# A fixed table for the issue order of all operations in an attention and FFN kernel on one core

## The chip, the cores and the metric

The kernel runs on one core of a Trainium2 chip. The metric is the device time in microseconds (us), median of three runs. A core has five engines with a queue each: TensorE (PE) for matrix products, VectorE (DVE), ScalarE (ACT), GpSimd (POOL), and SyncE (SP), which issues nearly all transfers here. An engine takes the instructions of its queue in order; between engines, semaphores hold an instruction back until what it reads is written and what it overwrites is read.

## What is computed

```python
def _attn_ref(q, k, v, tau):                      # 8 batches, 8 heads, 576 rows, head size 64
    scores = scale * np.matmul(q, k.transpose(0, 1, 3, 2))
    thresh = np.max(scores, axis=-1, keepdims=True) - tau
    scores = np.where(scores >= thresh, scores, -1000000000.0)
    scores = scores - np.max(scores, axis=-1, keepdims=True)
    attn = np.exp(scores)
    attn = attn / (np.sum(attn, axis=-1, keepdims=True) + 1e-09)
    return np.matmul(attn, v)
def _moe_ref(x, w_in, w_out, s, b):               # 4608 tokens, 512 -> 2048 -> 512
    r = np.maximum(x @ w_in, 0.0)
    return (s * (r * r) + b) @ w_out
```

The attention's output, heads side by side, is the x of the second part (the FFN).

## The kernel before

**Tiling.** A visit is one pair of heads of one batch and one part u of its query rows: 256 rows (u = 0) or 256 and the last 64 (u = 1). There are 64 visits, four (the four pairs) for each part. A visit has four score tiles of 128 rows by 576 keys, and a fifth for the last 64 rows. When the four pairs of a part are through, their values are 256 tokens of x and one FFN block runs: 16 steps f of 128 hidden units each. The last rows of four batches make a block of their own, so there are 18 blocks.

**A score tile** (`tile_of`): PE writes the products into a PSUM bank pair s0 or s1 (L427 for the first 12 visits, L438 from then on, L416 and L449 for the last rows); DVE scales them and takes the minimum (L472), DVE or ACT adds tau to it (L480, L477), ACT takes the exponential into em (L483), DVE masks and sums (L486) and takes the reciprocal of the sum (L491), POOL multiplies by it (L494; the first four visits do it behind the values, L573 and L596). The probabilities are transposed on PE in the first eight visits (L509, L512, then ACT copies them to er, L521 and L524), on DVE and by transfers later (L543, L545, L562). The values are 20 products of er with V (L582) into the bank pv, taken to x by ACT (L595, L599).

**An FFN block**: ACT and DVE split x into a high and a low part (L696, L698). Step f has 12 products h (L712, entries from L715 in two halves for f = 0 and 15), then on ACT a relu, a square and a rounding (L719, L720, L722), on POOL the low part (L723), and the second product in two halves, o0 and o1, of three matmuls each (L729). Both weight matrices are split into parts once, in the first 130 us (`weights`, L657 to L671), from loads L621 and L624. The column sums that carry b are one product (L676).

**The order.** Nothing is issued while these functions run: each call of `plan.add` makes an entry of what it emits, on which engine, with an assumed duration, and with the entries that it depends on. There are 6381 entries (PE 1314, DVE 1317, ACT 1891, POOL 791, SP 1067, one empty), numbered as they are added, and the numbers are the same before and after. `Plan.run` (L131 to L162) then makes the order in which they are issued, and so each engine's queue. It runs a list scheduler over the assumed durations forward, backward and forward again (`ordered`, L164 to L240), permutes the first 779 places by the table FIRST (L30), and moves 136 entries by the table MOVES (L65). Then the entries are emitted in that order (L899 to L902); waits follow from what each reads and writes.

Of the kernel before, what the change touches and what calls it, by code (L numbers as in the profile page):

```python
# [22 lines left out]
ROUNDS = 2  # L23
# [6 lines left out]
FIRST = (  # L30
# [33 lines left out]
)  # L64
# [21 lines left out]
class Plan:  # L86
# [44 lines left out]
    def run(self):  # L131
# [7 lines left out]
        for k in range(ROUNDS):  # L139
# [5 lines left out]
            if k == ROUNDS - 1:  # L145
                break
# [797 lines left out]
```

## Time and profile before

| | us |
|---|---|
| median of three runs | 1210.88 |
| lowest and highest | 1210.82, 1211.03 |
| span of the profiled execution, first to last instruction | 1208.6 |
| PE busy with matmuls | 1191.3 |
| DVE, ACT, POOL busy | 798.0, 763.4, 696.4 |

The profile is of one execution. The end of a matmul in it is modelled and consecutive matmuls overlap, so how fast PE moves is read from the starts of its instructions, and a shown idle time is the least that was lost. In a row of the timeline "x12" is a run of twelve like instructions; in brackets stands the idle time of the engine ahead of the row and what ended it.

### The profile page before, as it was taken

What the parts mean: (1) busy time and instruction counts of PE and PEld (TensorE: products, weight loads), DVE (VectorE), ACT (ScalarE), POOL (GpSimd) and SP (SyncE); (2) the same over time, 40 slices, a digit from 0 to 9 for tenths busy, and PEclk for the clock granted to TensorE, in tenths of its full rate; (3) what the DMA queues carried; (4) which work ended last, traced back from release to release, by engine and by line L of the source; (5) the groups of instructions that cost most, each with busy time, mean ns of one, the idle gap of its engine ahead of it and who ended that gap; (6) DMA issues with size and microseconds to landing.
All of it is one profiled execution on the core that took longest, in us unless ns stands there. A gap on an engine that the chain in (4) does not pass through costs nothing.

```text
span 1208.6 us, 24492 instructions
## 1 busy us (share of the span) xinstructions
PE 1191.3 (99%) x7956; PEld 985.4 (82%) x7956; DVE 798.0 (66%) x2149; ACT 763.4 (63%) x1890; POOL 696.4 (58%) x806
## 2 busy tenths in 40 slices
PE   7899999999999999999999999999999999999998
PEld 5577778788888888888887888788888888888997
DVE  7988876677786866766776667667766676672011
ACT  6888756666666766656666666566666566663443
POOL 2467636666666775566575666566657566562210
PEclk9999999999999999999999999999999999999999
DMA  8742465877867877666767776667767666762000
GB/s 298 260 136 80 97 157 133 182 181 170 186 150 179 187 159 171 150 159 151 171 142 163 177 160 143 155 146 162 163 159 164 156 154 152 169 148 57 17 18 18
DMA packets 259393, 180.68 MB, mean 149 GB/s; under 512 B 83394, under 2 KB 238018, under 8 KB 259266
## 3 DMA queue, kind: packets, MB, share of 16 engines
q1 hardware_dynamic: 259120, 178.98, 62.8%
q8 instruction: 64, 1.05, 0.3%
q14 instruction: 63, 0.52, 0.1%
q10 hardware_dynamic: 146, 0.13, 0.0%
HBM read 87.03 MB, written 9.44 MB: 80 GB/s over the span
## 4 chain that ended last, share of the span: by engine, by line
PE 96%; DVE 2%; DMA 1%; issue 0%; ACT 0%; POOL 0%; DVEq 0%; ACTq 0%; POOLq 0%
PE h L712 35%; PE o L729 34%; PE pv L582 13%; PE s L438 9%; PE s L427 2%; PE s L449 1%; PE pv L509 1%; DVE s L472 1%; DMA w<-in_moe_w_out_dram 1%; DMA vb<-in_v_dram 0%; PE s L416 0%; PE pv L512 0%; PE h L820 0%; DVE tr L486 0%; DVE k L662 0%
## 5 line engine op out<-in xcount | busy, mean ns | idle before, releaser
L712 PE MATMUL h<-xh,w 128*128 128x256 f32 x2304 | 465.5, 284 | 1.0 <-ACT g L719 0.9
L712 PEld LDWEIGHTS h<-xh,w 128*128 128x128 f32 x2304 | 377.4, 190 | 20.4 <-issue 2.6
L729 PE MATMUL o<-w,gh 128*128 128x512 f32 x1152 | 366.5, 399 | 0.0
L472 DVE TENSOR_SCALAR_CACHE_REDUCE s<-s,nsc 128x576 f32<-128x576 f32 x288 | 234.5, 821 | 144.4 <-PE s L438 115.4
L712 PE MATMUL h<-xl,w 128*128 128x256 f32 x1152 | 325.2, 282 | 0.6 <-DVE xl L698 0.6
L723 POOL TENSOR_TENSOR gl<-g,gh 128x256 fp32r<-128x256 f32 x272 | 204.0, 752 | 207.9 <-ACT gh L722 190.1
L494 POOL TENSOR_SCALAR em<-em,st,zero 128x576 f32<-128x576 f32 x262 | 219.2, 837 | 139.3 <-DVE st L491 89.9
L486 DVE SCALAR_TENSOR_TENSOR em<-s,st,em 128x577 f32<-128x577 f32 x270 | 218.4, 810 | 94.3 <-ACT st L477 59.5
L483 ACT ACTIVATE em<-s,st 128x576 f32<-128x576 f32 x270 | 199.0, 738 | 79.5 <-DVE s L472 50.1
L729 PEld LDWEIGHTS o<-w,gh 128*128 128x128 f32 x1152 | 194.9, 189 | 37.4 <-issue 15.9
L729 PE MATMUL o<-w,gl 128*128 128x512 f32 x576 | 224.8, 390 | 0.0
L712 PEld LDWEIGHTS h<-xl,w 128*128 128x128 f32 x1152 | 219.0, 190 | 6.6 <-DVE xl L698 0.8
L719 ACT ACTIVATE g<-h 128x256 f32<-128x256 f32 x288 | 110.4, 383 | 177.6 <-PE h L712 160.1
L543 DVE STREAM_TRANSPOSE tr<-em 128x512 f32<-128x512 f32 x252 | 178.2, 707 | 51.0 <-POOL em L494 43.9
L403 POOL TENSOR_TENSOR k<-kr,k 64x576 fp32r<-64x576 f32 x104 | 149.4, 1438 | 53.2 <-ACT k L402 40.0
L582 PE MATMUL pv<-er,vb 128*64 128x256 f32 (+1 forms) x1280 | 170.9, 412 | 0.4 <-ACT er L524 0.4
L438 PE MATMUL s<-k 128*128 128x288 f32 x832 | 144.1, 296 | 0.0
L438 PEld LDWEIGHTS s<-k 128*128 128x128 f32 x832 | 127.9, 188 | 17.6 <-issue 2.1
L582 PEld LDWEIGHTS pv<-er,vb 128*64 128x64 f32 x1280 | 86.5, 137 | 68.0 <-issue 14.2
L722 ACT CAST gh<-g 128x256 fp32r<-128x256 f32 x288 | 115.7, 404 | 34.1 <-PE o L729 30.3
L729 PEld LDWEIGHTS o<-w,gl 128*128 128x128 f32 x576 | 108.2, 188 | 25.0 <-POOL gl L723 0.3
L720 ACT ACTIVATE g<-g 128x256 f32<-128x256 f32 x288 | 119.7, 417 | 4.2
(104 smaller groups left out, 909.8 us busy)
## 6 DMA issues: line engine op xcount, KB each, us to landing
er<-tr SPq DMA_DIRECT2D x448, 160.0 KB, 3.5
kr<-in_k_dram SPq DMA_DIRECT2D x116, 288.0 KB, 4.3
vb<-in_v_dram SPq DMA_DIRECT2D x128, 128.0 KB, 3.3
qr<-in_q_dram SPq DMA_DIRECT2D x56, 160.0 KB, 4.5
er<-tr SPq DMA_DIRECT2D x112, 80.0 KB, 2.3
w<-in_moe_w_in_dram SPq DMA_DIRECT2D x16, 512.0 KB, 6.3
w<-in_moe_w_out_dram SPq DMA_DIRECT2D x16, 512.0 KB, 7.2
out_dram<-oo SPq DMA_DIRECT2D x30, 256.0 KB, 2.7
```

Source lines behind the costliest of these rows:

```text
L403: pool((1500, 1500), lambda: nc.gpsimd.tensor_tensor(out=z()[D:P], in0=kr[D:P, j], in1=z()[D:P].bitcast(F32), op=ALU.subtract), rk + [("z" ...
L438: nc.tensor.matmul(flat[sk][:, S0 + hf * HS:S0 + (hf + 1) * HS], lazy["q"][:, x, j, qc], lazy["k"][:, j, cs], start=(x == 0), stop=(x == 1))
L472: dve((740, 875), lambda: nc.vector.tensor_scalar(out=ps[:, S0:S0 + S], in0=ps[:, S0:S0 + S], scalar1=nsc, scalar2=None, op0=ALU.mult, op1 ...
L483: act((632, 740), lambda: nc.scalar.activation(out=ev, in_=ps[:, S0:S0 + S], func=AF.Exp, bias=low, scale=-1.0), [sk, (ks_, 0, k_)], [em_k ...
L486: dve((742, 830), lambda: nc.vector.scalar_tensor_tensor(out=eb, in0=ps[:, S0:S0 + S + 1], scalar=limit, in1=eb, op0=ALU.is_le, op1=ALU.mu ...
L494: pool((795, 825), lambda: nc.gpsimd.tensor_scalar(out=ev, in0=ev, scalar1=share, scalar2=zero, op0=ALU.mult, op1=ALU.add), [em_k, (ks_, 4 ...
L543: nc.vector.transpose(out=to[:, :, 0:NQ].rearrange("p m c q -> p m (c q)"), in_=ev[:, 0:M].rearrange("p (m r) -> p m r", m=4))
L582: nc.tensor.matmul(ps[j * D:(j + 1) * D, 0:32 * nb], vb[r, n, j, c], er[r, n, j, 0:nb, 32 * c:32 * c + 32], start=(c == 0), stop=(c == 4))
L712: nc.tensor.matmul(ps, w[:, c, :], x[:, c, :], start=(c == 0 and i == 0), stop=(c == NC - 1 and i == 2))
L720: act((322, 417), lambda: nc.scalar.activation(out=g, in_=g, func=AF.Square), [f"g{k}"], [f"g{k}"], at)
L723: do((712, 740), lambda: eng.tensor_tensor(out=lo, in0=g, in1=hi.bitcast(F32), op=ALU.subtract), [f"g{k}", f"gh{n}"], [f"gl{n}"], at)
L729: nc.tensor.matmul(bank[f"o{t}"], a[:, ts_], w, start=(f == 0 and i == 0), stop=(f == NF - 1 and i == 2))
```

## The change

The scheduler, both tables and the constants that it used go. A table ORDER names all 6381 entries in the order in which they are issued, and `run` returns them so. The entries, their engines, shapes and buffers are the same.

```diff
-import heapq
...
-ROUNDS = 2
...
-FIRST = (
-    1, 2, 3, 0, 7, 8, 9, 12, 13, 15, 16, 17, 18, 19, 20, 4, 22, 21, 25, 11, 6, 24, 26, 29, 31, 30, 33, 35, 36, 75, 14,
...
-MOVES = (
-    (780, 779), (1990, 2018), (2006, 2019), (2007, 2020), (2012, 2021), (2013, 2022), (4900, 4918), (4915, 4919),
...
+ORDER = (
+    1, 9, 2, 8, 7, 13, 14, 15, 16, 17, 18, 19, 20, 21, 22, 23, 24, 3, 10, 12, 40, 11, 41, 49, 42, 50, 0, 43, 44, 51, 52,
+    57, 190, 192, 193, 194, 27, 29, 30, 45, 58, 60, 66, 59, 67, 61, 139, 68, 69, 141, 142, 53, 54, 46, 47, 48, 78, 79,
...
     def run(self):
-        ops = self.ops
-        after = [[] for _ in ops]
...
-        return [ops[n][3] for n in order]
-
-    def ordered(self, before, after, rank, busy, done, back):
...
+        at = {n: k for k, n in enumerate(ORDER)}
+        assert len(at) == len(ORDER) == len(self.ops)
+        assert all(at[d] < at[n] for n in at for d in self.ops[n][4])
+        return [self.ops[n][3] for n in ORDER]
```

By engine, the entries that have another place in their queue than before, and the farthest move in places: PE 653 of 1314, 11; DVE 651 of 1317, 17; ACT 1015 of 1891, 32; POOL 400 of 791, 9; SP 641 of 1067, 43. On PE the changes between products on a part of the array (L427, L449, L582) and on the whole are 186 before and 182 after. The ends of the queues are the same, on PE the last 144 entries.

Some stretches of the queues, by entry number, before and after:

| queue, about when in the trace of before | before | after |
|---|---|---|
| POOL, start | 7, 8, 0 | 8, 7, 0 |
| SP, about 17 us | 280, 594, 204, 300, 136, ... (80 stood early, 138 later) | 280, 138, 80, 528, 299, ... |
| DVE, 48 to 59 us | 229, 237, 311, 322, 325, 323, 189, 544, 326, 238, 545, 534, 547, 535, 537, 538, 245, 555, 247, 548, 249 | 229, 237, 303, 322, 323, 189, 534, 238, 325, 544, 545, 535, 326, 547, 537, 538, 548, 245, 311, 247, 249, 555 |
| ACT, 56 to 60 us | 244, 246, 248, 541, 557, 344, 543, 252 | 244, 329, 246, 248, 541, 341, 543, 344, 557, 252 |
| PE, 56 to 61 us | 243, 554, 540, 250, 542, 251, 550, 258 | 243, 554, 540, 542, 250, 251, 550, 258 |
| PE, 133 to 148 us | 477, 497, 498, 780, 783, 512, 513, 961, 520, 518, 793, 519, 794, 801 | 498, 780, 477, 783, 512, 513, 961, 520, 497, 518, 793, 794, 519, 801 |
| PE, 213 to 217 us | 906, 1332, 1103, 1110, 1340 | 1103, 905, 898, 1110, 906, 1340 |

What they are: 7 the ones and zeros of PE's first products (L796, L797) and 8 the identity (L799); 80, 138 loads of V for visits 1 and 2 (L379, L382); 143, 196, 30, 303, 326 weight steps on DVE (L660, L662), 311 one of L671, 325 one of L660; 229 and 237 the masks L486 of the last tiles of visit 3 and 238 its reciprocal L491; 189 and 245 the values' scaling L596 of visits 2 and 3; 534, 544, 555 scale steps L472 of visit 4; 547, 537 its masks, 548 a reciprocal; 243 the values of visit 3, 244 its copy L595; 246, 248 the high parts L696 and 247, 249 the low parts L698 of the first block; 250, 251 the halves of its first product; 540, 542, 550 transposes L509 and L512 of visit 4, 541 and 543 their copies; 240 and 242 the last transpose of visit 3 and its copy L524; 780 a transpose L512 and 783 the values of visit 7; 477, 497, 498, 518, 519, 898, 905, 906 second-product halves L729; 520 the column sums L676; 793 and 794 the halves of the second block's first product and 801 its next product; 1103 and 1110 two products of the third block.

## Rows read from the trace of the kernel before

**Rows 1.** The page's first part: busy us of each engine, share, instructions.

```profile
PE 1191.3 (99%) x7956; PEld 985.4 (82%) x7956; DVE 798.0 (66%) x2149; ACT 763.4 (63%) x1890; POOL 696.4 (58%) x806
```

**Rows 2.** Busy time by stage: stretch, us, busy of PE, PEld, DVE, ACT, POOL, clock, DMA.

```profile
0.00:58.00 58.00, 46.48 (x291) 30.93 (x291) 49.56 (x141) 42.67 (x85) 20.18 (x29) 0.97 0.87 288
12.50:55.50 43.00, 35.59 (x245) 23.33 (x244) 42.90 (x118) 36.97 (x77) 16.27 (x13) 0.96 0.93 304
150.00:1150.00 1000.00, 999.53 (x6741) 837.23 (x6740) 659.46 (x1783) 625.07 (x1570) 612.36 (x706) 1.00 0.68 153
```

**Rows 3.** Timeline of PE in an undisturbed stretch: start, us, engine, line, operation, tiles, count.

```profile
605.80 0.63 PE L729 MATMUL o<-w,gh 128*128 128x512 f32 x2
...
606.49 0.28 PE L712 MATMUL h<-xh,w 128*128 128x256 f32 x1
...
607.93 0.63 PE L729 MATMUL o<-w,gh 128*128 128x512 f32 x2
```

**Rows 4.** Waits of PE's products from 58 us on: us in total, times, longest.

```profile
PE h L712 <- ACT g L719: 0.9, 2, 0.5
```

**Rows 5.** Timeline of PE, 134 to 149 us.

```profile
136.62 3.06 PE L582 MATMUL pv<-er,vb 128*64 128x320 f32 x20 [0.40 <-ACT er L524]
...
143.03 0.96 PE L729 MATMUL o<-w,gh 128*128 128x512 f32 x2
...
144.30 0.38 PE L712 MATMUL h<-xh,w 128*128 128x256 f32 x1
...
146.41 0.28 PE L712 MATMUL h<-xh,w 128*128 128x256 f32 x1
147.16 0.38 PE L712 MATMUL h<-xh,w 128*128 128x256 f32 x1 [0.47 <-ACT g L719]
```

**Rows 6.** Timeline of DVE, 49 to 53 us.

```profile
49.36 0.69 DVE L671 TENSOR_TENSOR bias_t<-bias_t,k 128x512 f32<-128x512 f32 x1
49.96 0.76 DVE L660 TENSOR_SCALAR k<-k 128x512 int32<-128x512 int32 x2
...
52.30 0.69 DVE L662 SCALAR_TENSOR_TENSOR k<-w,k 128x512 int32<-128x512 int32 x1
52.92 0.17 DVE L491 RECIPROCAL st<-st 128x4 f32<-128x4 f32 x1
```

**Rows 7.** Timeline of ACT, 52.8 us: the last copy of visit 3.

```profile
52.84 0.27 ACT L524 COPY er<-pv 64x128 f32<-64x128 f32 x1
```

**Rows 8.** Timeline of PE at the first FFN product.

```profile
57.89 0.36 PE L712 MATMUL h<-xh,w 128*128 128x256 f32 x1
58.88 0.39 PE L712 MATMUL h<-xl,w 128*128 128x256 f32 x1 [0.63 <-DVE xl L698]
```

**Rows 9.** Timeline of POOL at the start: the identity's first step, and what follows it.

```profile
1.13 0.21 POOL masks.py:197 MEMSET k<- 128x128 f32 x1
...
1.64 0.53 POOL L786 MEMSET bias_t<- 128x512 f32 x1
```

**Rows 10.** Timeline of PE, values of visits 0 and 1; the page's median landing of V loads.

```profile
22.70 2.48 PE L582 MATMUL pv<-er,vb 128*64 128x256 f32 x20
...
33.51 1.12 PE L573 MATMUL pv<-k,st 128*64 128x128 f32 x8
...
vb<-in_v_dram SPq DMA_DIRECT2D x128, 128.0 KB, 3.3
```

**Rows 11.** The page's costliest groups: count, busy us, mean ns, idle before.

```profile
L472 DVE TENSOR_SCALAR_CACHE_REDUCE s<-s,nsc 128x576 f32<-128x576 f32 x288 | 234.5, 821 | 144.4 <-PE s L438 115.4
L486 DVE SCALAR_TENSOR_TENSOR em<-s,st,em 128x577 f32<-128x577 f32 x270 | 218.4, 810 | 94.3 <-ACT st L477 59.5
L483 ACT ACTIVATE em<-s,st 128x576 f32<-128x576 f32 x270 | 199.0, 738 | 79.5 <-DVE s L472 50.1
```

**Rows 12.** Busy time in two stretches of the front, columns as in rows 2.

```profile
28.00:32.00 4.00, 2.09 (x17) 1.50 (x15) 4.00 (x13) 3.60 (x9) 2.87 (x3) 1.00 0.96 284
32.00:35.50 3.50, 3.50 (x22) 2.49 (x21) 3.50 (x7) 1.73 (x5) 0.00 (x0) 0.51 0.65 196
```

More of the change, by code (lines that the diff above doesn't have):

```diff
@@ L29 @@
 SCALED_LATE = 4
-FIRST = (
[33 rows of a table removed]
-)
-MOVES = (
[17 rows of a table removed]
+ORDER = (
[326 rows of a table added]
 )
 class Plan:
-    HANDOVER, TO_PE = 50, 150
-    PASS, OVER = 100, 400
-    TURN, NEAR = 95, 8000
-    SPARE = {"DVE": 100, "ACT": 100, "POOL": 100, "SP": 300}
-    SHARE, LATER, STRETCH, EARLY = 0.7, 1.0, 1.3, 75e3
     def __init__(self):
@@ L117, in banks @@
         return [k] if k in ("s0", "s1", "pv", "o0", "o1") else ["h"] if k in ("h0", "h1") else []
-    def free_at(self, n, t, last, tail, hand):
-        for b, writes in self.ops[n][8]:
-            for e, wrote, at, rest in last.get(b, ()):
-                if e != self.ops[n][0] and (writes or wrote):
-                    t = max(t, at + (rest if tail is None else tail) + hand)
-        return t
-    def used(self, n, at, rest, last):
-        for b, writes in self.ops[n][8]:
-            was = last.get(b, []) if not writes else []
-            last[b] = [u for u in was if u[1] or u[0] != self.ops[n][0]] + [(self.ops[n][0], writes, at, rest)]
@@ L131, in run @@
-    def run(self):
-        ops = self.ops
-        after = [[] for _ in ops]
-        for n, o in enumerate(ops):
-            for d in o[4]:
-                after[d].append(n)
-        before = [o[4] for o in ops]
-        rank, early = [o[5] for o in ops], set()
-        for k in range(ROUNDS):
-            more = [(self.SHARE if n in early else self.LATER) * self.SPARE.get(o[0], 0) +
-                    (self.STRETCH - 1) * o[1] * (o[0] == "PE" and n in early) for n, o in enumerate(ops)]
-            busy = [o[1] + s for o, s in zip(ops, more)]
-            done = [o[2] + s for o, s in zip(ops, more)]
-            order = self.ordered(before, after, rank, busy, done, False)
-            if k == ROUNDS - 1:
-                break
-            early = {n for t, n in order if t < self.EARLY}
-            end = {n: t + done[n] for t, n in order}
-            last = max(end.values())
-            back = self.ordered(after, before, [last - end[n] for n in range(len(ops))], busy, done, True)
-            start = {n: -t - done[n] for t, n in back}
-            rank = [start[n] for n in range(len(ops))]
-        order = [n for _, n in order]
-        order[:len(FIRST)] = [order[k] for k in FIRST]
-        moved = [(to, order[k]) for k, to in MOVES]
-        gone = {n for _, n in moved}
-        order = [n for n in order if n not in gone]
-        for to, n in moved:
-            order.insert(to, n)
-        at = {n: k for k, n in enumerate(order)}
-        assert len(at) == len(ops) and all(at[d] < at[n] for n in at for d in before[n])
-        return [ops[n][3] for n in order]
@@ L164, in ordered @@
-    def ordered(self, before, after, rank, busy, done, back):
-        ops = self.ops
-        left = [len(b) for b in before]
-        ready = [0.0] * len(ops)
-        free, coming, there = {}, {}, {}
-        for n, o in enumerate(ops):
-            free[o[0]] = 0.0
-            coming.setdefault(o[0], [])
-            there.setdefault(o[0], [])
-            if not left[n]:
-                heapq.heappush(coming[o[0]], (0.0, n))
-        order, port, mode, last = [], 0.0, False, {}
-        def delay(n, t):
-            at = max(t, port) if ops[n][6] else t
-            if not ops[n][8]:
-                return at - t
-            hand = self.TO_PE if ops[n][0] == "PE" else self.HANDOVER
-            return self.free_at(n, at, last, done[n] - busy[n] if back else None, hand) - t
-        for _ in ops:
-            best = None
-            for e in free:
-                t = free[e]
-                while coming[e] and coming[e][0][0] <= t:
-                    n = heapq.heappop(coming[e])[1]
-                    heapq.heappush(there[e], (rank[n], n))
-                if not there[e]:
-                    if not coming[e]:
-                        continue
-                    t = coming[e][0][0]
-                if best is None or t < best[0]:
-                    best = t, e
-            t, e = best
-            while coming[e] and coming[e][0][0] <= t:
-                n = heapq.heappop(coming[e])[1]
-                heapq.heappush(there[e], (rank[n], n))
-            n = heapq.heappop(there[e])[1]
-            if e == "PE" and mode and not ops[n][7]:
-                for at, m in sorted(there[e]):
-                    if ops[m][7] and at < rank[n] + self.NEAR:
-                        there[e].remove((at, m))
-                        heapq.heapify(there[e])
-                        heapq.heappush(there[e], (rank[n], n))
-                        n = m
-                        break
-            wait = delay(n, t)
-            if wait > self.PASS:
-                for at, m in sorted(there[e]):
-                    if delay(m, t) <= self.PASS and busy[m] < wait + self.OVER:
-                        there[e].remove((at, m))
-                        heapq.heapify(there[e])
-                        heapq.heappush(there[e], (rank[n], n))
-                        n, wait = m, delay(m, t)
-                        break
-            t += wait
-            if e == "PE":
-                t += self.TURN * (mode != ops[n][7])
-                mode = ops[n][7]
-            if ops[n][6]:
-                port = t + busy[n]
-            if ops[n][8]:
-                self.used(n, t + busy[n], done[n] - busy[n], last)
-            order.append((t, n))
-            free[e] = t + busy[n]
-            for u in after[n]:
-                if ops[u][0] == e == "PE":
-                    late = busy[n]
-                else:
-                    late = busy[n] + done[u] - busy[u] if back else done[n]
-                    p = n if back else u
-                    late += 0 if ops[u][0] == e else self.TO_PE if ops[p][0] == "PE" else self.HANDOVER
-                ready[u] = max(ready[u], t + late)
-                left[u] -= 1
-                if not left[u]:
-                    heapq.heappush(coming[ops[u][0]], (ready[u], u))
-        order.sort()
-        return order
```

372 rows, old and new, of tables (FIRST, MOVES, ORDER) are left out of this document.

## The prediction

> **What bounds the kernel now.** I read the page's busy line first: TensorE (PE) has matmuls running for 1191.3 of 1208.6 us, the other engines are at 66% and less [rows 1]. So only time in which PE does not run at its own pace can be won by an order, and the second view, busy time by stage, says where that is: up to 58 us PE is busy for 46.5 of 58.0 us, from 150 to 1150 us for 999.5 of 1000 [rows 2]. Third, the pace: in an undisturbed stretch the starts follow one another by 0.69 us for half of a second FFN product, 1.44 for a first product [rows 3]; no order changes these. Fourth, the list of waits behind 58 us: PE waits for ScalarE's L719 twice, 0.9 us together [rows 4]; beside it stand two waits of 0.6 and 0.4 us, which come below. The middle has therefore almost nothing to give, and the question is what the table does at a handful of places, and whether it opens new waits.
>
> Before 58 us the reader has to look at VectorE (DVE), not PE. From 12.5 to 55.5 us it is busy for 42.9 of 43.0 us [rows 2], and the FFN cannot start before the first four visits have passed through it; PE's stalls there are shadows of that chain. After 58 us everything to the end is PE work of fixed length. So the end moves by (1) how far the first FFN product moves, (2) the PE waits behind it that vanish, (3) those that appear. The median of the runs is 1210.88 us and the profiled execution's span 1208.6; I work on the span and keep the 2.3 us outside it.
>
> **Behind 58 us, what vanishes.** Four places, each read as start-to-start minus the pace.
> - 783, values of visit 7: PE is idle for 0.40 us because L582 waits for the last ScalarE copy (L524) of the transposes just ahead of it [rows 5]. In the new order 477, a second-product half of 0.69 us, stands between transpose 780 and 783. It covers the wait: 0.40.
> - 518 and 793 around the column sums (520, L676): 518 starts at 143.03 and 793 at 144.30, 1.27 us for a half worth 0.69, so 0.58 are lost [rows 5]. The new order puts 497 as well (0.69) between. Unknown is how much of the 0.58 is the full-precision sum itself still draining: bounds 0 and 0.58, I take 0.45, since the next consumer of the bank (793) is the one that stalls.
> - 801 behind 794: the last start of 794 at 146.41 and the first of 801 at 147.16, 0.75 where 0.12 is the spacing, so 0.63, released by L719 [rows 5]. In the new order 519 (0.69) stands between instead of ahead of 794: covered, 0.63.
> - 1110 directly behind 1103 at 216 us: the other of the two waits of [rows 4], also 0.63. The new order has 905 and 898 between, 1.38: covered.
> Sum 2.1 us, bounds 1.7 and 2.4. The work that moved there comes from places where it covered nothing I can find. PE changes between tiled and whole-array products 182 times instead of 186, worth under 0.1 us each by the same spacing; I count nothing.
>
> **The front.** The first FFN product needs the values of visit 3 (243, L573 and L582), whose last condition is the reciprocal 238 (L491 at 52.92 us); the last ScalarE copy 242 ends with it, at 53.10 [rows 6, 7]. On DVE the new table takes 311, 325, 326 and 544 from ahead of 238 and puts 534 there: by their spacing 0.60 + 0.38 + 0.62 = 1.60 us earlier, 544 and 534 being alike [rows 6]. But the copies hang on the mask 237, and only 303 (a step like 326, 0.62) leaves from ahead of it. So 243 moves by 0.6 to 1.5 us; I take 1.0, as two more DVE steps that release transposes (189, L596) also move. Then 247, the low part that 250 waits 0.99 us for (57.89 to 58.88 [rows 8]): 555 leaves from ahead of it (0.82, the L472 of [rows 11]), 311 enters (0.60) but starts at once, because 555 stood waiting for its scores; I take 0.5, bounds 0.2 and 1.0. Against this, transpose 542 now precedes 250, and needs a ScalarE copy that queues behind both casts L696: 0 to 0.6, I take 0.4. Sum: 1.1.
> What is late at the very start: GpSimd makes the identity (8) before the ones and zeros (7) that PE's first products read. The identity's two steps take from 1.13 to 1.64 us [rows 9], so PE starts up to 0.5 us later; the products that only keep PE busy shrink that if the first scores wait for their loads anyway. Between 0 and 0.5, I take 0.3. A weight step (30) now fills a DVE gap near 12 us, but 143 and 196 come earlier as well, so nothing is booked for it.
> SP: many loads change places. The one to fear is 138, a small load that must wait until the values of visit 0 are through PE, and that now stands ahead of 80, a V load of visit 1 that waits for nothing. The wait ends when L582 of 22.70 us is through, 80 is needed by L573 at 33.51 us, and such a load lands in 3.3 us [rows 10]. Covered by some 4 us or more even on full queues; if the queue behind 138 took all of it, values of visit 1 would be late, on a path with DVE work enough to hide some of it. I take 0, bound 1.
> Front: 1.1 - 0.3 = 0.8, bounds -0.5 and 2.0.
>
> **What appears.** The new order turns some buffers faster. A score bank passes DVE L472, ScalarE L483 and DVE L486 before PE may write it again, 0.82 + 0.74 + 0.81 = 2.37 us plus handovers [rows 11]. By the pace of [rows 3], the shortest PE work between two uses of a bank is 4.0 us in the old order, with no wait on it; in the new one it is 3.3, 3.5, 3.5 and 3.7 us, and some 20 turnarounds lie at 4.7 us or below where there were about 10. Second-product halves that reuse a gh/gl buffer have 1.4 us of PE work twice. First products follow each other no closer than 0.8 us (one pair at 0.2 stands in both orders), and 0.7 ran free. I take 0.2 us, bounds 0 and 6 (the last below).
>
> **Sum.** 2.1 + 0.8 - 0.2 = 2.7 us: span 1205.9, median 1208.2. By the bounds of the late places and the front, 1210.88 - 4.4 = 1206.5 to 1210.88 - 1.7 + 0.5 + 1.0 = 1210.7, without the slow rival.
>
> **Rivals.**
> *The front does not move.* Identity first, 542 and the ScalarE copies eat what DVE gives; only the late gain stays: 1210.88 - 2.1 + 0.2 + 0.5 = 1209.5. For it: ScalarE's copies end as late as the reciprocal [rows 7]. Against: both casts and masks come earlier too.
> *More.* Front 2.0 and late 2.4: 1206.5. For it: every one of the first FFN steps has 0.1 to 0.3 us of slack that is counted nowhere here.
> *The clock falls at the wrong place.* PE ran at 0.51 of its clock, the lower of its two levels (1.2 GHz), from 32.0 to 35.5 us, after a stretch of 4.00 us in which it was busy for 2.09; DVE was busy throughout, so that cost nothing [rows 12]. Gaps at the front will lie elsewhere now. If such a stretch falls on the first FFN steps, where PE is the path, half of 3.5 us is lost: 1208.2 + 1.75 = 1209.9. The Trainium skill, page "TensorE: Matmul & The Clock Gate", section "HAM oscillation — how this bites in real kernels", says that idle gaps drop the array to half rate and the next work starts cold; the trace agrees with the 0.51. By that rule alone this rival would be the likelier the more the front is rearranged.
> *Slower.* The faster score banks. DVE runs its transposes (L543, L545) in front of a scale step L472; if it is behind by more than the 1.0 us that a 3.3 us turnaround leaves, PE waits at each of the 20 short ones. From 0.27 us on each that undoes the gain and 0.2% more; at 0.3, 6 us: 1208.4 + 5.8 = 1214.2. For it: DVE's slack is not PE's to choose. Against: none of the short turnarounds of the old order waits, and DVE is busy 66% there [rows 1, 4].
> That the table does nothing new is excluded: half of the entries change places on their engine.
>
> **How the numbers follow.** Forecast 0.50, of which its own range 1207.4 to 1209.2; more 0.14; front unmoved 0.17; clock 0.08; slower 0.11. What a measurement of this kernel can tell is about 0.2%, 2.4 us, so "faster" begins below 1208.46: 0.32 of the forecast and all of "more", 0.46. "Same" takes 0.18 of the forecast, the unmoved front and the clock, 0.43. Slower 0.11. The range 1205.6 to 1212.0 takes in the bounds and leaves out most of the slow rival and the far end of "more".
>
> **What would show it.** In the changed kernel's waits of PE behind 58 us, the two for L719 and the one for L524 are gone and no score line (L438, L449) has idle time ahead of it. The first L712 starts near 57 us, its second start follows without a gap, and the reciprocal ahead of visit 3's L573 lies near 51.5 us. PE's first start lies near 1.7 us. I am wrong if the first L712 stands at 58 or later, if the granted clock is below 1 behind 55 us, or if DVE L472 or L486 releases PE in the middle.

## The result, and the profile after

The changed kernel is slower: 1226.25 us median (1224.03 to 1227.5, four runs) against 1210.85 us of the kernel before beside it; ratio 1.0125, 95% interval 1.0111 to 1.0139. The prediction was 1208.2 us, 1205.6 to 1212.0. The profiled execution of after took 1227.5 us with a span of 1225.2. In its kernel every line number is 149 higher than before (L712 is L861, L562 is L711, L402 is L551).

First the page: its busy line and its chain of the work that ended last (shares of the span).

```profile
PE 1196.3 (98%) x7956; PEld 987.8 (81%) x7956; DVE 807.7 (66%) x2149; ACT 755.4 (62%) x1890; POOL 698.7 (57%) x806
...
PE 78%; DVE 6%; DMA 6%; SPq 4%; ACT 3%; issue 2%; POOL 1%; DVEq 0%; ACTq 0%; POOLq 0%
```

The chain before:

```profile
PE 96%; DVE 2%; DMA 1%; issue 0%; ACT 0%; POOL 0%; DVEq 0%; ACTq 0%; POOLq 0%
```

The instructions are as many as before [rows 1], but the chain is another: before, nearly all of it was PE; now it leaves PE for DMAs, SP's queue (SPq) and DVE. Where, the stages of [rows 2] tell (stretch, us, busy of PE, PEld, DVE, ACT, POOL, clock, DMA share, GB/s).

```profile
0.00:58.00 58.00, 44.46 (x268) 29.65 (x270) 49.86 (x133) 40.01 (x80) 18.52 (x27) 0.85 0.80 265
12.50:55.50 43.00, 34.66 (x220) 22.46 (x219) 41.52 (x105) 33.74 (x70) 14.55 (x11) 0.83 0.76 249
150.00:1150.00 1000.00, 990.19 (x6656) 826.61 (x6655) 663.14 (x1791) 612.01 (x1557) 607.70 (x704) 1.00 0.68 154
```

Both parts lose. In the front the first FFN product comes late (timeline of PE; [rows 8] answers it):

```profile
62.42 0.36 PE L861 MATMUL h<-xh,w 128*128 128x256 f32 x1
62.62 0.28 PE L861 MATMUL h<-xl,w 128*128 128x256 f32 x1
```

The first start has gone from 57.89 to 62.42 us. That is not all lost, since the other half no longer waits ahead of it; by the start of entry 251, the later half before, it is 59.60 to 63.21, 3.6 us. The last second product (6365) starts at 1215.04 us, 16.6 later than before. So the front costs 3.6 and all behind it 13.0, where the prediction had a gain of 0.8 and one of 1.9.

In the middle PE waits for things that it did not wait for before (us in total, times, longest; [rows 4] answers the first line):

```profile
PE h L861 <- ACT g L868: 3.8, 4, 1.4
PE pv L731 <- DMA er<-tr: 1.5, 2, 0.9
PE s L587 <- DVE em L635: 1.4, 4, 0.4
PE s L598 <- DVE em L635: 1.1, 2, 0.6
PE pv L731 <- issue: 1.0, 1, 1.0
```

The list names less than what is lost, since ends of products are modelled. By start-to-start minus the pace of [rows 3], a dozen places make up most of it: around 185 to 195 us (values 1044 and 1089), 465, 577 to 603, 615, 637, 786, 820, 975, 1030 and 1069 us. One of them, followed back along the chain (start, us, what):

```profile
581.62 0.53 SPq L507
...
582.20 0.59 SPq L528
...
582.84 0.64 SPq L504
...
583.59 5.68 DMA kr<-in_k_dram
...
589.34 0.04 ACT k L551
...
589.92 0.39 ACT g L868
...
590.35 1.70 PE h L861 x12
```

And ACT's timeline at that place (in brackets the idle time before, and what ended it):

```profile
585.83 0.72 ACT L632 ACTIVATE em<-s,st 128x576 f32<-128x576 f32 x1
589.34 0.67 ACT L551 CAST k<-kr 128x576 fp32r<-128x576 f32 x1 [2.79 <-DMA kr<-in_k_dram]
589.92 0.38 ACT L868 ACTIVATE g<-h 128x256 f32<-128x256 f32 x1
```

And SP's wait between 574 and 579.4 us:

```profile
SPq L711 <- DVE tr L694: 5.4, 1, 5.4
```

The reader should see two queues in a row. On SP a store of a transposed tile (L711) stands at the head and waits 5.4 us for DVE. Then two more stores, the Q load (L507), a V load and two K loads are issued one right behind the other, some 0.6 us each. The buffer of the second K load was free at 580.7 us, when POOL's L552 ended; it goes at 583.59 and takes 5.68 us, where the page's median for such loads is 4.4. On ACT the cast of these K rows stands ahead of the activation of an FFN step. The last matmul of the product that the activation reads started at 587.46 us, but the activation starts at 589.92, behind the cast, and PE waits for it. In both waits the engine does nothing, and what stands behind the head of its queue is held up.

How often that happens is seen in the waits of ACT and DVE for DMAs, 150 to 1150 us. Before:

```profile
ACT k L405 <- DMA qr<-in_q_dram: 9.7, 17, 1.2
...
ACT k L402 <- DMA kr<-in_k_dram: 4.8, 8, 0.9
...
DVE tr L543 <- DMA er<-tr: 3.6, 3, 1.7
```

After:

```profile
ACT k L554 <- DMA qr<-in_q_dram: 20.7, 14, 3.5
...
DVE tr L692 <- DMA er<-tr: 18.0, 13, 3.5
...
ACT k L551 <- DMA kr<-in_k_dram: 16.6, 21, 2.8
```

The casts wait 37.3 us instead of 14.5, and DVE's transposes, which may not overwrite a tile until its store to er has landed, 18.0 instead of 3.6. Set entry by entry from both traces: the 560 stores behind 60 us go out 1605 us (summed) after they could, against 961 before, and 30 of them are issued less than 6 us before PE first reads them, against 1. The shortest such lead of a V load falls from 10.8 to 3.0 us.

Two theories go into the experiments. Theory Q: the loss comes from in-order queues, SP's above all, in which an entry that waits holds up loads and stores. Rival C: it comes from the order of the computing engines itself, score banks that turn too fast (the slow rival of the prediction) above all.

### The profile page after: what moved, and what is told of

Its sections match the earlier page's. It is cut to its first block, busy times and chain, and to the rows that moved or that the text cites. A ratio compares the mean times of both kernels' runs of the same rounds, so it can differ in the third digit from the quotient of the medians.

```text
span 1225.2 us, 24324 instructions
## 1 busy us (share of the span) xinstructions
PE 1196.3 (98%) x7956; PEld 987.8 (81%) x7956; DVE 807.7 (66%) x2149; ACT 755.4 (62%) x1890; POOL 698.7 (57%) x806
## 4 chain that ended last, share of the span: by engine, by line
PE 78%; DVE 6%; DMA 6%; SPq 4%; ACT 3%; issue 2%; POOL 1%; DVEq 0%; ACTq 0%; POOLq 0%
PE h L861 28%; PE o L878 26%; PE pv L731 11%; PE s L587 8%; DMA er<-tr 2%; DMA qr<-in_q_dram 2%; PE s L576 2%; SPq L711 2%; PE s L598 1%; DVE s L621 1%; DVE em L635 1%; ACT em L632 1%; DVE tr L692 1%; DVE bias_t L820 1%; SPq L507 1%
## 5 line engine op out<-in xcount | busy, mean ns | idle before, releaser
L861 PE MATMUL h<-xh,w 128*128 128x256 f32 x2304 | 465.7, 284 | 3.9 <-ACT g L868 3.8
L861 PEld LDWEIGHTS h<-xh,w 128*128 128x128 f32 x2304 | 377.5, 190 | 26.9 <-ACT g L868 7.7
L861 PE MATMUL h<-xl,w 128*128 128x256 f32 x1152 | 325.2, 282 | 0.0
L643 POOL TENSOR_SCALAR em<-em,st,zero 128x576 f32<-128x576 f32 x262 | 222.1, 850 | 164.8 <-DVE st L640 104.0
L635 DVE SCALAR_TENSOR_TENSOR em<-s,st,em 128x577 f32<-128x577 f32 x270 | 219.1, 814 | 118.7 <-ACT em L632 61.0
L868 ACT ACTIVATE g<-h 128x256 f32<-128x256 f32 x288 | 109.9, 382 | 204.4 <-PE h L861 173.8
L861 PEld LDWEIGHTS h<-xl,w 128*128 128x128 f32 x1152 | 219.0, 190 | 6.7
L552 POOL TENSOR_TENSOR k<-kr,k 64x576 fp32r<-64x576 f32 x104 | 148.9, 1434 | 40.4 <-ACT k L551 22.6
L587 PEld LDWEIGHTS s<-k 128*128 128x128 f32 x832 | 124.7, 188 | 22.3 <-issue 7.4
```

The costliest lines, as they stand in the source:

```text
L552: pool((1500, 1500), lambda: nc.gpsimd.tensor_tensor(out=z()[D:P], in0=kr[D:P, j], in1=z()[D:P].bitcast(F32), op=ALU.subtract), rk + [("z" ...
L587: nc.tensor.matmul(flat[sk][:, S0 + hf * HS:S0 + (hf + 1) * HS], lazy["q"][:, x, j, qc], lazy["k"][:, j, cs], start=(x == 0), stop=(x == 1))
L635: dve((742, 830), lambda: nc.vector.scalar_tensor_tensor(out=eb, in0=ps[:, S0:S0 + S + 1], scalar=limit, in1=eb, op0=ALU.is_le, op1=ALU.mu ...
L643: pool((795, 825), lambda: nc.gpsimd.tensor_scalar(out=ev, in0=ev, scalar1=share, scalar2=zero, op0=ALU.mult, op1=ALU.add), [em_k, (ks_, 4 ...
L861: nc.tensor.matmul(ps, w[:, c, :], x[:, c, :], start=(c == 0 and i == 0), stop=(c == NC - 1 and i == 2))
```

## The experiments

Each kernel is the changed one with another table ORDER. A diff here is of the queues: for each engine, which order its entries have. "new" is the changed table, "old" the one before. Between the engines any sequence that keeps each queue and all dependences gives the same program.

**SP against the rest.** Old order on SP alone, and new order on SP alone.

```diff
 PE, DVE, ACT, POOL: new
-SP: new
+SP: old
```

> The new order on PE, DVE, ACT and POOL, the old order on SP's queue alone (641 of its 1067 entries go back). Theory Q (the loss comes from the loads and stores that SP issues in order, one waiting entry holding up those behind it): the loss of 15.4 us goes nearly all, 1207 to 1213 us, first FFN product near 58 us, no waits of PE on a transposed store or on the scale steps in the middle. Rival C (the loss comes from the order of the four computing engines, score banks that turn too fast above all): 1222 to 1227 us as in the changed kernel. Between, 1214 to 1221, both.

```diff
-PE, DVE, ACT, POOL: new
+PE, DVE, ACT, POOL: old
 SP: new
```

> The old order on PE, DVE, ACT and POOL, the new order on SP's queue alone. Theory Q: 1220 to 1230 us, first FFN product near 61 us or later, PE waits in the middle on stores of the transposes and on scores. Rival C: 1210 to 1213 us, no more than the old kernel. If both this one and the one with SP's old order are slow, what costs is that the two orders do not fit each other, not either alone.

Measured: 1237.83 us (1.0225, 1.0207 to 1.0243) and 1315.36 us (1.0881, 1.0852 to 1.0910). Both are slower than the changed kernel. So the question as put has no answer: SP's order is neither good nor bad, it fits an order of the computing engines or it does not. The second run shows how much hangs on it: nothing but the sequence of loads and stores is changed, and it costs 105 us. The granted clock falls with it: 0.97 in the mean from 150 to 1150 us, 1.00 before and in the changed kernel. Its waits for DMAs, 150 to 1150 us:

```profile
DVE tr L692 <- DMA er<-tr: 77.8, 24, 8.6
...
ACT k L551 <- DMA kr<-in_k_dram: 30.8, 20, 4.0
```

**Front against middle.** The cut is the first FFN product (250).

```diff
-all engines: new
+all engines: new up to 250 (319 entries), old behind
```

> The new order up to the first FFN product (entry 250, 319 entries on all engines), behind it the old order. Theory Q with two separate places: the first FFN product is 3.6 to 4.5 us late and the middle, with the old queue, loses nothing more: 1214 to 1216 us. Rival: the late front alone sets the loads out of step and the middle loses with it: 1220 us and more.

```diff
-all engines: new
+all engines: old up to 250 (313 entries), new behind
```

> The old order up to the first FFN product, behind it the new order. Theory Q with two separate places: the front is as before (58 us), the middle loses its 13 us: 1221 to 1225 us. Rival, the middle suffers only from the late front: 1207 to 1211 us.

Measured: 1214.58 us (1.0030, 1.0019 to 1.0042) and 1225.45 us (1.0122, 1.0107 to 1.0137). The first is clean: its PE starts are 3.5 us late at 73 us and 3.5 us late at 1198 us, so the old middle neither wins nor loses behind a late front. The second has the old front (251 at 60.72 us; in the seven traces with the old front it starts between 59.60 and 60.74, and the trace of before is the earliest) and is 14.7 us slower, with its PE waits at nearly the same places as the changed kernel. The middle loses this without a late front. The two do not add up (3.8 and 14.7 against 15.4): behind the old front the middle loses some 3 us more than behind the new one, and why was not tested.

**SP without waiting entries.** On the kernel with the old front.

```diff
 PE, DVE, ACT, POOL: old up to 250, new behind
-SP: the same
+SP: behind 60 us, an entry that could not go yet steps aside for the next that could
```

> As the run with the old front and the new middle (1225.45 us), on PE, DVE, ACT and POOL unchanged; on SP's queue behind 60 us an entry that is not yet free to go (by the times at which the work that it waits for ended in that run's trace) steps aside for the next one that is; 815 of the 1067 entries change places. Theory Q (entries that wait hold up loads and stores behind them, and the compute engines that consume those in order pass the delay on to PE): 1208 to 1214 us, the waits of PE behind 150 us gone or nearly so. Rival C (the order of the computing engines has the waits in itself): 1222 to 1227 us, the same waits.

Measured: 1218.22 us (1.0059, 1.0045 to 1.0072). That lies between the two expectations: SP's order alone gives 7.2 of the 14.7 us back, half of what theory Q wanted. It is not a gain that this rule would bring to any kernel, since the middle of before has only 0.5 us to win [rows 2]. The waits show which half:

```profile
ACT k L551 <- DMA kr<-in_k_dram: 17.8, 21, 2.2
...
ACT k L554 <- DMA qr<-in_q_dram: 16.5, 14, 3.1
...
DVE tr L692 <- DMA er<-tr: 0.2, 1, 0.2
```

DVE no longer waits for stores (16.0 us in the run that this one was made from), the stores go out 903 us (summed) behind their time, and PE has no wait for L635, that is for a score bank, behind 150 us. But ACT's casts still wait 34.3 us. SP's total waiting is no measure of this: its stores wait for the transposes' last step 182.9 us here and 168.4 us in the changed kernel. What counts is what stands behind the waiting entry.

**ACT and POOL without waiting entries**, on top of that, and alone.

```diff
 PE, DVE: old up to 250, new behind; SP: as in the run above
-ACT, POOL: old up to 250, new behind
+ACT, POOL: from 150 to 1190 us, an entry without its input steps aside for one that could run
```

> As the run in which SP's entries step aside (1218.22 us), and besides, on ACT and POOL from 150 to 1190 us, an entry whose input had not come by its turn steps aside for a later one that could run (539 of ACT's and 138 of POOL's entries change places; PE, DVE and SP as there). If the half of the loss that was left comes from casts of K and Q rows at the head of ACT's queue that wait for their loads (34 us of such waits there, longest 3.1, against 14.5 us, longest 1.2, in the kernel before): those waits fall under 15 us and the time to 1211 to 1214 us. If it comes from PE's own order or from score banks that turn faster: 1217 to 1220 us.

```diff
 PE, DVE, SP: old up to 250, new behind
-ACT, POOL: the same
+ACT, POOL: as above, by this kernel's own trace
```

> As the run with the old front and the new middle (1225.45 us), SP's queue as it is there, but on ACT and POOL from 150 to 1190 us entries whose input had not come step aside (542 and 148 entries change places). SP's order gave 7.2 us back by itself, this edit 4.0 us on top of it. If the two are separate: 1220.5 to 1222.5 us, DVE's waits for the stores (16 us) stay. If ACT's and POOL's order is the root and SP's only a symptom: 1213 to 1217 us. If it only works with SP's: 1224 to 1227 us.

Measured: 1214.2 us (1.0026, 1.0016 to 1.0035) and 1220.06 us (1.0072, 1.0057 to 1.0087). The edit gives 4.0 us on top of SP's and 5.4 us alone, so the two are separate causes and add up within the intervals: 7.2 + 5.4 against 11.25 together. In the second, DVE still waits 16.0 us for stores, as expected. The casts' waits did not fall under 15 us but only to 27.2 us in the first; what fell is what stood behind them: PE's waits for POOL's split of K (L552) went from 2.0 us to none, those for the activation L868 from 2.0 to 1.4 us. PE's busy time from 150 to 1150 us, in the kernel with the old front, with SP's edit, and with both:

```profile
150.00:1150.00 1000.00, 991.12 (x6639) 827.93 (x6636) 661.14 (x1785) 610.48 (x1554) 605.58 (x700) 1.00 0.68 154
```

```profile
150.00:1150.00 1000.00, 994.66 (x6692) 830.50 (x6689) 660.14 (x1785) 613.86 (x1562) 608.36 (x703) 1.00 0.68 153
```

```profile
150.00:1150.00 1000.00, 997.88 (x6719) 834.29 (x6718) 658.82 (x1785) 618.29 (x1563) 610.52 (x705) 1.00 0.68 153
```

**The same rule once more.**

```diff
-SP, ACT, POOL: as in the run with both edits
+SP, ACT, POOL: step aside again, by that run's trace
```

> As the run in which SP, ACT and POOL step aside (1214.2 us), the same rule once more by that run's own trace (193 entries of ACT, 50 of POOL, 107 of SP). If what is left there is still entries that wait at the head of a queue: 1210.5 to 1213 us. If it lies in PE's own new order: 1213.5 to 1215 us.

Measured: 1216.7 us (1.0043, 1.0026 to 1.0060), no better: the median is 2.5 us higher, and the intervals overlap. Neither expectation holds; whether the last 3 us lie in PE's new order or in a better fit of the queues stays open.

**The front: SP's wait.** Entries 138 and 137 wait for the values of visit 0. The prediction feared 138, ahead of 80.

```diff
 SP, new front: ... 280,
-138, 80, 528, 299, 203, 339, 319, 137, 204, 300, 136, ...
+80, 528, 299, 203, 339, 319, 204, 300, 138, 137, 136, ...
```

> As the run with the new front and the old middle (1214.58 us), but on SP's queue the loads 138 and 137, which wait for the values of visit 0, stand behind 80, 528, 299, 203, 339, 319, 204 and 300 (in the new table 138 stands ahead of all of them and SP waits from 17.1 to 27.6 us for it). If that wait makes the front late: first FFN product back by 2 to 3.5 us, 1211 to 1212.5 us. If the front is late by the clock (0.50 from 10 to 16 us) or by the order on DVE: 1214 to 1215 us.

Measured: 1214.26 us (1.0025, 1.0015 to 1.0035), and in the profile the first FFN product moves by 0.01 us. SP's timeline around 138 (L531), with the new front and then with this edit:

```profile
16.53 0.33 SPq L773 DMA_DIRECT2D w<-in_moe_w_out_dram  x1
27.05 0.60 SPq L531 DMA_DIRECT2D vb<-in_v_dram  x1
```

```profile
17.06 0.43 SPq L528 DMA_DIRECT2D vb<-in_v_dram  x1
18.36 0.50 SPq L524 DMA_DIRECT2D k<-in_q_dram  x1
```

Ten microseconds in which SP issues nothing cost nothing here, since no load behind 138 is needed sooner: with the new front 80 lands at 29.9 us, and its first reader on PE starts at 33.5 us, with the edit as well.

**The front: the start and the clock.** With the new front the row of the granted clock reads 0.50 from 10 to 16 us, the lower of the two levels; before, it reads 1.00.

```diff
-POOL: 7, 8, ...
+POOL: 8, 7, ...       (all else old)
```

> The old order, except that GpSimd makes the identity (8) ahead of the ones and zeros (7), as in the new table; PE starts 0.5 us later. If the later start is taken up by the wait for the first loads: 1210.6 to 1211.1 us, the clock 1.00 up to 20 us. If it is what lets the clock fall to its lower level from 10 to 16 us, as in both runs with the new front: 1211.5 to 1213 us, with 0.5 in the rows of that stretch.

```diff
-all engines: new up to 250, old behind
+all engines: old up to 96, new up to 250, old behind
```

> As the run with the new front and the old middle (1214.58 us), but the first 15 us (all up to the first scores of visit 1, entry 96) in the old order. If the front is late because the clock falls to its lower level at 10 to 16 us, and that hangs on how PE starts: clock 1.00 there, first FFN product near 58.5 us, 1210.5 to 1211.5 us. If the order on DVE and ACT behind 15 us makes it late: 1213.5 to 1215 us.

```diff
-all engines: old
+all engines: new up to 96, old behind
```

> The other half: the new order in the first 15 us only (up to entry 96; DVE's weight step 30 ahead of 58, the identity first, K1 behind w2 on SP), everything behind in the old order. If the clock does it: 0.50 from 10 to 16 us, 1213.5 to 1215 us. If it is the order behind 15 us: 1210.7 to 1211.7 us.

Measured: 1211.29 us (1.0002, 0.9993 to 1.0011), 1215.83 us (1.0042, 1.0027 to 1.0057) and 1210.42 us (0.9999, 0.9989 to 1.0008). That row misleads, though: the records of the granted clock begin at 15.0 us in the trace of before, at 14.5 us with the old start and at 6.6 us in the changed kernel, and ahead of the first record the row shows 1.00. What PE's steps take tells the level. Before, and with the old start:

```profile
13.12 1.06 PE L509 MATMUL h<-k,em 128*128 128x128 f32 x4
...
17.10 0.60 PE L509 MATMUL h<-k,tr 128*128 128x128 f32 x4
```

```profile
13.20 1.06 PE L658 MATMUL h<-k,em 128*128 128x128 f32 x4
```

In the changed kernel four such transposes take 1.11 us at 12.77. So all three run this stretch at the lower level, and these runs compare no levels. What they do show: PE beginning 0.5 us later, alone or with the new start (1.75 and 1.76 us), costs nothing that can be told from zero, and the old start does not make the new front faster. The clocks differ behind 15 us: the changed kernel is at the lower level for 12.0 us there (to 16.8, from 20.2 to 23.6 and from 40.7 to 47.5 us), the kernel before for 3.5 (32.0 to 35.5). What that costs is read below; what lets the clock fall there was not settled.

**The front: DVE.** What is left is the order behind 15 us.

```diff
 PE, ACT, POOL, SP: new up to 250, old behind
-DVE: the same
+DVE: old
```

> As the run with the new front and the old middle (1214.58 us), but DVE's order is the old one throughout (69 entries go back); PE, ACT, POOL and SP keep the new front. If DVE's order makes the front late: first FFN product near 58.5 us, 1210.5 to 1211.5 us. If PE's, ACT's or the start does: 1213.5 to 1215 us.

Measured: 1220.78 us (1.0080, 1.0065 to 1.0095), against both expectations. As with SP, the old order of one engine does not fit the new order of the others: DVE now stands without work for 4.5 us ahead of visit 3's reciprocal, and two of its weight steps take 1.76 us instead of 0.69. So the question was put to single steps. In the kernel with the new front, DVE and POOL between 45 and 50 us:

```profile
46.20 1.50 DVE L809 TENSOR_SCALAR k<-k 128x512 int32<-128x512 int32 x1
47.62 1.76 DVE L811 SCALAR_TENSOR_TENSOR k<-w,k 128x512 int32<-128x512 int32 x1
...
45.63 1.79 POOL L817 TENSOR_TENSOR w<-k,w 128x512 fp32r<-128x512 f32 x1 [1.28 <-ACT w L815]
47.38 1.45 POOL L817 TENSOR_TENSOR w<-xh,w 128x512 fp32r<-128x512 f32 x1
```

A weight step of DVE that starts while POOL runs one of its own takes until POOL's is over: 1.50 us for one that takes about 0.4 [rows 6], 1.76 for one that takes 0.69. There are three such steps ahead of visit 3's reciprocal, 3.2 us in all; the old order has none. DVE is also idle once, 1.17 us up to 23.5 us, waiting for scores of visit 1. Two things can make these late: two weight steps (143, 196) stand ahead of the scale steps of visit 1, and PE is at the lower level of its clock from 19.6 to 23.0 us, where four transposes take 1.12 us and the scores 1.88 (0.66 and 1.24 before).

```diff
 DVE, new front: ... 126, 90,
-87, 95, 170, 178, 171, 151, 179, ...
+170, 178, 95, 171, 87, 151, 179, ...
 ... 305, 291,
-302, 306, 226, 234, 227, 235, 229, 237, 303, ...
+226, 234, 227, 235, 229, 237, 302, 306, 303, ...
```

> As the run with the new front and the old middle (1214.58 us), but on DVE five weight steps move by a few places so that they no longer start beside one of GpSimd's weight steps L817: 87 and 95 behind the scale steps 170 and 178, 302 and 306 behind the exponent steps 229 and 237. In that run three such steps took 1.50, 1.76 and (two together) 2.37 us, where they take 0.42, 0.68 and 1.28 without it: 3.2 us in all. If that stretching is what DVE loses: the steps take their short times, 1211.8 to 1213 us (the places that they give up leave DVE 0.4 and 1.3 us without work). If it costs nothing on the path: 1214 to 1215 us.

```diff
 DVE, new front: ... 142, 31,
-143, 196, 97, 105, 98, 70, 106, 100, 108, 145, ...
+97, 105, 98, 70, 106, 100, 108, 143, 196, 145, ...
```

> As the run with the new front and the old middle, but DVE's weight steps 143 and 196 stand behind 108 again and not ahead of the scale steps 97 and 105 of visit 1. If their 1.0 us ahead of 97 delay the next scores (113) and leave DVE 1.17 us without work at 23.5 us: that gap closes, 1213.3 to 1213.9 us. If not: 1214.2 to 1215 us.

Both edits at once:

> Both edits of DVE's order at once. If the stretched steps and the gap are separate losses that add up and make most of the 3.6 us: 1210.8 to 1212 us. If either only moves the loss on: 1212.5 us and more.

Measured: 1213.91 us (1.0022, 1.0013 to 1.0032), 1214.6 us (1.0026, 1.0015 to 1.0037) and 1214.25 us (1.0024, 1.0015 to 1.0033). The medians hardly tell these apart from 1214.58, so no more than 0.7 us of the front comes back. The profiles show what moved, but each is one execution: the first and the last took 1212.61 and 1212.73 us, 1.3 and 1.5 below their medians, the second 1215.16, 0.6 above its own, and the one with the new front alone 1213.93, 0.65 below. The two steps with 302 and 306 moved:

```profile
47.06 0.83 DVE L621 TENSOR_SCALAR_CACHE_REDUCE s<-s,nsc 128x576 f32<-128x576 f32 x1 [1.55 <-PE s L576]
...
50.40 0.42 DVE L809 TENSOR_SCALAR k<-k 128x512 int32<-128x512 int32 x1
50.74 1.29 DVE L811 SCALAR_TENSOR_TENSOR k<-w,k 128x512 int32<-128x512 int32 x2
```

The steps are short again, 0.42 and 1.29 for two, but in the place that they left DVE waits 1.55 us for the next scores, which PE makes at the lower level here (1.88 us at 45.15, 1.39 before). Added up along DVE's queue from its step 58 to visit 3's reciprocal (238), each against before in us, from the traces:

```
kernel                    start of 58   idle   stretched   work    reciprocal 238
new front, old middle       -0.48      +1.17     +3.24    -1.55       +2.38
 ... weight steps moved     -0.67      +3.12      0       -1.30       +1.15
 ... 143 and 196 back       -1.00      +2.71     +3.24    -1.31       +3.63
 ... both                   -0.91      +3.48      0       -1.29       +1.27
 ... old start              +0.07      +0.86     +3.22    -1.09       +3.06
changed kernel              -0.28      +1.45     +3.23    -1.44       +2.95
```

The columns add up to the last one ("work" is what is left over). So the new table does take some 1.5 us of DVE work out of the path. It loses 1.2 to 1.5 us of idle time and 3.2 us of stretched steps, and where one is taken away part of it comes back as the other.

How much of that is the clock, two of these kernels show in part. With 143 and 196 back and with both edits the order is the same on every engine until 33 us. Busy time and clock (third number from the end) in the one and in the other, and DVE's scale step 114 in both:

```profile
15.50:18.00 2.50, 2.50 (x13) 1.56 (x9) 1.52 (x4) 0.55 (x2) 0.00 (x0) 0.50 1.10 330
15.50:18.00 2.50, 1.46 (x11) 0.77 (x7) 2.04 (x8) 1.75 (x5) 0.00 (x0) 1.00 1.10 330
```

```profile
23.82 0.82 DVE L621 TENSOR_SCALAR_CACHE_REDUCE s<-s,nsc 128x576 f32<-128x576 f32 x1
```

```profile
22.49 0.82 DVE L621 TENSOR_SCALAR_CACHE_REDUCE s<-s,nsc 128x576 f32<-128x576 f32 x1
```

The first is at the lower level until 18.4 us and again from 21.8 to 25.2, the second until 15.2. (In the first the gap up to 23.5 us is gone, and gaps of 0.98 and 1.05 us stand ahead of 16.6 and 19.5 us instead.) Their steps 58 start within 0.1 us of each other, their steps 114 are 1.33 us apart. With the order the same, that is the clock's doing, so it does cost the front where DVE waits for PE's scores. How much of the changed kernel's loss it makes, no run settles.

**The late places alone**, in the old kernel. (477 and 898, which the new table has there, can't go behind 780 and 1103 with the other queues as they were; 498 and 905 stand for them.)

```diff
 PE, old: ...
-497, 498, 780, 783, ..., 520, 518, 793, 519, 794, 801, ..., 905, ..., 1103, 1110, ...
+780, 498, 783, ..., 520, 497, 518, 793, 794, 519, 801, ..., 1103, 905, 1110, ...
```

> The old order, except for four second-product halves on PE: 498 behind transpose 780, 497 behind the column sums 520, 519 behind 794, 905 behind 1103. Nothing else changes. My prediction's late term: the four waits of 0.40, 0.45, 0.63 and 0.63 us vanish, 2.1 us in all, 1208.4 to 1209.2 us. Rival, the waits move to the next PE step or the moved half is missed where it stood: 1210.3 to 1211 us.

Measured: 1210.05 us against 1211.1 beside it (0.9992, 0.9983 to 1.0000), between the two expectations. In its profile the starts gain 0.26 us at 783, 0.27 at the column sums and 801, and 0.33 behind 1110, 0.86 in all. Instead of [rows 5] PE's timeline has at 783:

```profile
137.37 3.06 PE L731 MATMUL pv<-er,vb 128*64 128x320 f32 x20 [0.61 <-ACT er L673]
```

The wait has grown from 0.40 to 0.61 us: transpose 780, now ahead, waits itself for ACT, and the last copy comes hardly sooner. Behind 1110 the next first product (1117) loses 0.29. This is the only kernel of the study whose interval does not go above 1.0000; the gain is at the edge of what its measurement can tell.

## Why the prediction was wrong

**The step that failed** is "The middle has therefore almost nothing to give, and the question is what the table does at a handful of places, and whether it opens new waits", with the answer 0.2 us (bounds 0 and 6) for new waits. That [rows 2] shows 999.5 of 1000 us says that nothing can be won there. It says nothing of what can be lost, and I looked for losses only in the buffers that PE itself turns over, the score banks above all. Measured, the middle loses 13.0 us, for the greater part by entries that wait at the heads of SP's, ACT's and POOL's queues: in the kernel with the old front, which is 14.7 us slower, 7.2 us go with SP's order alone and 5.4 us with ACT's and POOL's alone. Some 3 us are not explained.

**The row that should have been read** is the list of waits of ACT, not of PE: before, ACT's casts already wait 25 times for their loads, up to 1.2 us each, with no harm to PE. That is a plan with little slack left in its K and Q loads, and of a table that moves 641 of SP's 1067 entries the first question is what stands behind each entry that waits. The prediction asked it for one entry.

**Slower, by the score banks**: 1214.2 us at 0.11. The sign was right and the mechanism not. PE does wait for L635 in the changed kernel (6 times, 2.5 us from 150 us on). With the old front these waits are 2 and 0.8 us, and none is left once SP's entries step aside, with DVE's and PE's orders unchanged: there they were a consequence.

**The front**: predicted -0.8, measured +3.6 against the trace of before (+2.5 to +3.6 against the seven with the old front). DVE's work ahead of 238 fell by some 1.5 us, where the sum had 1.0 (0.6 to 1.5). What was wrong is that DVE would stay as busy as in [rows 2] and its steps as long as in [rows 6]. Three steps run long beside POOL's, 3.2 us in all, and DVE waits 1.2 to 1.5 us for scores, where 143 and 196 stand earlier ("so nothing is booked for it") and PE's clock is at its lower level. The long steps could have been read from the trace of before, though not in its front; DVE, and POOL beside it:

```profile
118.81 1.71 DVE L662 SCALAR_TENSOR_TENSOR k<-w,k 128x512 int32<-128x512 int32 x1
...
118.71 1.27 POOL L668 TENSOR_TENSOR w<-k,w 128x512 fp32r<-128x512 f32 x1 [3.49 <-ACT w L666]
```

That these losses make the front late is added up along DVE's queue; the edits that should have taken them away gave back 0.7 us at most in the medians, so it is not shown by a run.

**SP at the start**, 0 with a bound of 1: 0, as reasoned. I had counted some 4 us of cover between the landing of 80 and its use; in the changed kernel it lands at 30.6 us and is first read at 34.1, although SP stood for 10.5 us.

**GpSimd's order at the start**, 0.3 between 0 and 0.5: PE does start 0.5 us later, and alone it is not told from zero (+0.2, interval -0.8 to +1.3 us).

**The late places**: 2.1 us predicted, 0.86 by the profile and 1.05 by the median when done alone. The mechanism stands; the size is too large because I took each half that moves as full cover. What moves into a gap leaves another place, and the step that it moves past (780) had a wait of its own. In the changed kernel, where 477 stands in that gap, 783 gains 0.47 us (predicted 0.40), the column sums and 801 together 0.35 (predicted 1.08).

**The clock**: behind 58 us it is 1.00, so the rival as put, the lower level on the first FFN steps, did not come. It came at another place: on PE's scores of visit 1, for which DVE then waits. The prediction saw the lower level cost nothing in the one stretch of before in which DVE was busy throughout [rows 12], and priced it only where PE is the path.

**The bounds** do not follow from their terms: the late places add up to at most 2.2 us, not 2.4, and the front to -1.3 and 2.5, not -0.5 and 2.0. With these the range would not have reached 1226 us either.

## What to carry to other kernels

An order that keeps a bound engine busy says nothing of how close the other queues are to holding it up: before a queue of loads is reordered, set for each load how long before its use it lands, and see what stands behind each entry that waits. Orders of several in-order queues belong together; going back on one of them (SP's, DVE's) was slower than either whole. And where a term is taken as a gain because an engine was busy throughout, ask what filled its gaps, since that is what a new order may move away. A row of the granted clock is worth as much as the records behind it: where the trace has none yet, read the level from what a step of known shape takes.

## What the runs showed of the hardware

The long DVE steps were not expected. Weight steps of DVE with int32 operands that take 0.42 and 0.69 us alone took 1.50 and 1.76 us beside POOL's L817 and ended within 0.6 us behind it; POOL's own step, behind DVE's L820, took 1.79 us where others take 1.27. The Trainium skill, page "SBUF — State Buffer", section "SBUF: two separate sides", says that VectorE and GpSimd have one pair of ports in common, that a VectorE step in a 2-port mode, or with two SBUF inputs beside a GpSimd step that reads SBUF, and a GpSimd step hold it for their whole instruction, and that whichever comes second blocks. By that rule a step is not slowed but begins late, which the trace agrees with: the times over are 1.08 and 1.07 us, and 1.22 and 1.21 us were left of POOL's step. L811 and L820 have two SBUF inputs; L809 has one, and no run here shows in which mode it ran.

With the same order of all engines up to there, DVE's step 114 started at 23.82 us in a kernel whose granted clock was 0.50 until 18.4 us and from 21.8 to 25.2, and at 22.49 us in one where it was 0.50 until 15.2.

SP's queue stood for 10.5 us with nothing issued and the end did not move by what the profile can show, while the same loads in a sequence that does not fit cost 105 us.
